# Regrouping the low parts of a Strassen pair's differences, with x's scaling and two weight pieces moved, in a float32 attention and SwiGLU kernel on one NeuronCore

## The chip, the cores and the metric

One core of a Trainium2 chip runs the whole program. The metric is the device time of one execution, in microseconds (us). The kernel before took 1289.45 us, the median of 3 runs (1287.16 to 1290.14).

## What is computed

Two stages follow each other. First, channel attention on q, k and v, each 2 x 6016 x 256 (float32): the columns of q and k are normalised over the 6016 rows, a 256 x 256 score matrix per batch is softmaxed, and v is multiplied by it. Then every one of the 12032 rows of 256 is scaled by its root mean square, multiplied by two 256 x 1536 matrices, gated and projected back:

```
s = kn.T @ qn / tau ; a = softmax(s) ; x = v @ a
xn  = x / rms(x) * rms_g
out = (silu(xn @ w_gate) * (xn @ w_val)) @ w_out
```

Each float32 operand is split into a high part (fp32r) and a low part (the difference to it), and each product is three matmuls: high by high, high by low, low by high.

## The kernel before

**Blocks and steps.** The 12032 rows are worked in 24 blocks (j) of 512 (two are shorter). Blocks 0 and 1 run while scores, norms and weights are still being prepared. A block has 12 steps (f), one per 128 of the 1536 hidden columns; two steps make a pair p = f // 2. From block 2 on, the two matrices into the hidden layer are multiplied by a Winograd scheme of seven products per step, and one step's products are spread over three steps of the program: `emit_step` (from L737) issues for the step two back (`old`) products 7, 2 and 4, for the one before products 3 and 6, and for the new one products 5 and 1. So TensorE's (PE's) order in a step is 7, 2, 3, 6, 5, 1, first half of an output projection, 4, second half. All matmuls of the seven are at L730. A PSUM tile `pu` holds products until VectorE (DVE) and ScalarE (ACT) have read it, and there are three.

**What the other engines do in a step.** ACT copies parts of `pu` into `t` (L766, L771), applies Silu in even steps (L775, L796). DVE adds `pu`, `pq` and `t` into `zg` (even step) or `zv` (odd step) at L759 and L760. In odd steps DVE multiplies gate by value: three quarters at L779, the last quarter, which is product 4, at L788. Then `round_pair` (L653) queues the roundings: ACT makes the high part (L692), GpSimd (POOL) the low part by subtraction (L698). `zg` has two buffers, so a pair's L759 writes over the tile of the pair before the last.

**Turned pairs.** In blocks 4 to 22 the pairs 2, 3 and 4 take the output projection by Strassen's scheme. Their `zg` has four quarters. Three are rounded at once (`gx`); then `run_turned` (L681) makes four differences in place on DVE (L684), in the order quarter 0, 3, 2, 1, after POOL has read the quarters for `gx`. At the start of the next odd step `run_later` (L701) rounds the four differences in two groups, `gy` (quarters 0 and 1) and `gz` (quarters 2 and 3). `G` lists which group's half goes with which weight in the output projection (`emit_out_turned`, L893), which follows about five steps behind. For pair 5, which follows the turned pair 4 and ends in step 1 of the next block, the flag `late` (L777) puts the product of three quarters behind that of the last one, at L790.

**x for the next blocks.** While a block runs, the next block's x is turned by DVE blocks of 32 (L511) and 16 small DMAs on SyncE's (SP's) queue (L520), scaled by `rms_g` on ACT (`scale`, L530), combined on POOL (`parts`, L541 and L546) and rounded in two rounds (`hi` and `rest`, ACT L558 and POOL L560). Tables written by hand (`turn0` to `turn4`, `steady`, with `_mid` and `_pre`) say after which step each is issued: `steady` serves blocks 5 on, `turn2` block 2. `at(j, f, ...)` adds single jobs at the end of a step: softmax pieces of the second batch, and building the Winograd weights (`build_s(p, piece)`: piece 0 and 1 sums and differences on DVE, L578 and L587; 2 rounding on ACT, L590; 3 low parts on DVE, L593). `at_step` holds their steps, counted from block 1's start; those that fall into block 1 are issued inside `emit_hidden`, behind its DVE product at L830.

```
L777  late = old and odd and not strassen(j, f // 2) and strassen(j, f // 2 - 1)
L778  if old and odd and not late:
L779      nc.vector.tensor_tensor(out=zg[:, 1:], in0=zg[:, 1:], in1=z, op=ALU.mult)
L788      nc.vector.tensor_tensor(out=zg[:, 0], in0=u[:, 1], in1=zg[:, 0], op=ALU.mult)
L789      if late:
L790          nc.vector.tensor_tensor(out=zg[:, 1:], in0=zg[:, 1:], in1=z, op=ALU.mult)
```

Of the kernel before, what the change touches and what calls it, by code (L numbers as in the profile page):

```python
# [12 lines left out]
ALU = mybir.AluOpType  # L13
# [6 lines left out]
def kernel(  # L20
# [17 lines left out]
    nc = tc.nc  # L38
# [107 lines left out]
    for b, sizes in enumerate(([2] * 2 + [4] * 9 + [2] * 3 + [1], [CH] * 11 + [3])):  # L146
        t = 0
# [138 lines left out]
    def softmax_exp(b, c):  # L286
        z, mx = sm_t[b]
        nc.scalar.activation(
            out=z[:, c, :], in_=z[:, c, :], func=AF.Exp, scale=-1.0, bias=mx[:, c:c + 1],
            accum_out=mx[:, KC + c:KC + c + 1],  # L290
        )
# [26 lines left out]
    for b in range(B):  # L318
        t = 0
# [6 lines left out]
    B1 = NB // B  # L326
# [316 lines left out]
    rounds, subs, later, turned = [], [], [], []  # L643
# [6 lines left out]
    def by_quarter(t, n, h):  # L650
        return t[:, :n * h].rearrange("p (i n) -> p i n", i=n)

    def round_pair(j, p, zg, h):  # L653

        x, y = new_g("x", 3, j, 2 * p), new_g("y", 2, j, 2 * p + 1)
        engine = nc.vector if (j, p) == (NB - 1, NP - 1) else nc.gpsimd
        w = [[w[:, 2 * p + i, e * P:(e + 1) * P] for w in wo] for i in range(2) for e in range(2)]
        if strassen(j, p):
            z = new_g("z", 2, j, 2 * p + 1)
            a12, a22, a11, s4 = w  # L660
            s1, s2, s3 = ([s[:, PAIRS.index(p), m * P:(m + 1) * P] for s in so_hl] for m in range(3))
            turned.append(zg)
            rounds.append((zg[:, :3], *(by_quarter(t, 3, h) for t in x), engine))
            later.append((zg[:, :2], *(by_quarter(t, 2, h) for t in y), engine))
            later.append((zg[:, 2:], *(by_quarter(t, 2, h) for t in z), engine))
            q = [[t[:, i * h:(i + 1) * h] for t in x] for i in range(3)]
            r = [[t[:, i * h:(i + 1) * h] for t in g] for g in (y, z) for i in range(2)]
            G[j, 2 * p] = [(2, 0, a11, q[0]), (0, 0, a12, q[1]), (0, h, s4, q[2])]
            G[j, 2 * p + 1] = [
                (1, 0, a22, r[1]), (2, h, s2, r[2]), (3, h, s1, r[0]), (3, 0, s3, r[3]),  # L670
            ]
        else:
            rounds.append((zg[:, 1:3], *(by_quarter(t, 2, h) for t in x), engine))
            later.append((zg[:, 0:4:3], *(by_quarter(t, 2, h) for t in y), engine))
            for i, g in enumerate((x, y)):
                if j == NB - 1:
                    G[j, 2 * p + i] = g
                    continue
                G[j, 2 * p + i] = [(e, 0, w[2 * i + e], [t[:, :2 * h] for t in g]) for e in range(2)]
# [7 lines left out]
    def strassen(j, p=PAIRS[0]):  # L687
        return STRA <= j < NB - 1 and p in PAIRS
# [48 lines left out]
    def emit_step(j, f, odd, outs=(), pre=(), mid=()):  # L737
# [5 lines left out]
        now, mid_, old = (flight + [None] * 3)[:3]  # L743
# [3 lines left out]
        if old:  # L747
            j, f, h, product, u, t = old
# [3 lines left out]
            if f % 2 == 0:  # L752
                z = pool["z"].tile([P, 4 * HN], F32, tag="zg", name=f"zg_{j}_{f}")
# [20 lines left out]
        if old and not odd:  # L774
            nc.scalar.activation(out=zg[:, 1:], in_=zg[:, 1:], func=AF.Silu)  # L775
            run_turned()
        late = old and odd and not strassen(j, f // 2) and strassen(j, f // 2 - 1)  # L777
        if old and odd and not late:  # L778
            nc.vector.tensor_tensor(out=zg[:, 1:], in0=zg[:, 1:], in1=z, op=ALU.mult)  # L779
        for go in mid:  # L780
            go()
# [3 lines left out]
        if old:  # L785
            product(4, u[:, 1])
            if odd:
                nc.vector.tensor_tensor(out=zg[:, 0], in0=u[:, 1], in1=zg[:, 0], op=ALU.mult)  # L788
                if late:  # L789
                    nc.vector.tensor_tensor(out=zg[:, 1:], in0=zg[:, 1:], in1=z, op=ALU.mult)  # L790
                round_pair(j, f // 2, zg, h)
                del zs[j, f // 2]
                run_rounds()
                run_subs()
            else:
                nc.scalar.activation(out=zg[:, 0], in_=u[:, 1], func=AF.Silu)  # L796
# [168 lines left out]
    with tc.manual_schedule():  # L965
# [128 lines left out]
        def at(j, f, go):  # L1094
            extra.setdefault((j, f), []).append(go)
# [39 lines left out]
        at(1, 0, lambda: join_squares(1, 1))  # L1135
        at(1, 1, end_scores)
        at_step = [(2 * p + 2, 2 * p + 3, 2 * p + 4, 2 * p + 4) for p in range(NP - 3)]
        at_step += [(8, 9, 10, 12), (13, 14, 15, 16), (16, 18, 19, 20)]
        for i in (2, 3, 0, 1):
            for p in range(NP):  # L1140
                j, f = divmod(NF + at_step[p][i], NF)
# [20 lines left out]
        at(3, 3, lambda: keep_norms(1))  # L1162
        at(5, 2, lambda: softmax_min(1, 0))
        at(6, 2, lambda: softmax_min(1, 1))
        at(7, 2, lambda: (softmax_exp(1, 0), softmax_exp(1, 1)))
        at(B1 - 2, 2, lambda: softmax_div(1, 0))
        at(B1 - 2, 2, lambda: softmax_div(1, 1))

        steps = [(j, f) for j in range(NB) for f in range(NF)]
        owed = []  # L1170
# [21 lines left out]
        def xn(h):  # L1192
            return lambda n: emit_xn(n, h)
# [7 lines left out]
        def of(m, go):  # L1201
# [16 lines left out]
        load = of(3, load_v)  # L1218

        steady = {  # L1220
            1: (s0, scale),
            3: (hi, v1),
            4: (sums_, c0, c1),
            5: (s1,),
# [8 lines left out]
        turn4 = {  # L1233
            **steady,
            1: (v0, s0),
            3: (scale, v1),
            4: (parts, hi, c0, c1),
            5: (rest,),
# [12 lines left out]
            11: (m0, m1),  # L1251
        }
        turn3_mid = {5: (parts,), 7: (x0, q0, r0), 9: (x1, q1), 11: (n1,)}
        turn2_mid = {**turn3_mid, 0: after(1, xn(1))}
        turn2 = {
            **turn3,
            0: after(1, xm(0), xm(1)),
            4: (scale, s0),
            6: (v1,),
            8: (rest,),  # L1260
        }
        turn1 = {
# [96 lines left out]
```

## Time and profile before

| | before |
|---|---|
| median of 3 runs | 1289.45 us (1287.16 to 1290.14) |
| the profiled execution | 1290.91 us, span of its trace 1289.1 us |
| busy: PE, weight loads, DVE, ACT, POOL | 1265.8, 1200.5, 919.2, 853.6, 802.5 us |
| PE's mean granted clock | 0.997 |

The durations below come from the profiled execution. PE's matmuls overlap in the record, so a group of six is shown as one span that is longer than six times the pitch; the end of each is modelled. "Idle" on the weight-load row (PEld) is the time in which the next load waited.

### The profile page before, as it was taken

How to read it: one execution, taken by the hardware profiler on the slowest of the kernel's cores; microseconds unless marked ns; L12 is line 12 of the kernel's file. 1: busy time of each engine (PE TensorE's matmuls, PEld its weight loads, DVE VectorE, ACT ScalarE, POOL GpSimd, SP SyncE). 2: the span in 40 equal slices, each digit the busy share in tenths (PEclk: the TensorE clock that was granted, in tenths of full speed). 3: DMA queues.
4: the chain of work that ended last, by engine and by line, in shares of the span. 5: the costliest groups of instructions: out<-in, count | busy, mean ns of one | idle time of the engine just before them, and what ended most of it. 6: DMA issues, size and time to landing. Idle time of an engine off the chain costs nothing.

```text
span 1289.1 us, 25061 instructions
## 1 busy us (share of the span) xinstructions
PE 1265.8 (98%) x9225; PEld 1200.5 (93%) x9225; DVE 919.2 (71%) x1573; ACT 853.6 (66%) x1771; POOL 802.5 (62%) x639
## 2 busy tenths in 40 slices
PE   8999998999999999999999999999999999999998
PEld 7789987999999999999999999999999999999998
DVE  5789696658667767767777776677677676677664
ACT  5577546666767677666666766766766766766654
POOL 0120254665777777777777766776776776776652
PEclk9999999999999999999999999999999999999999
DMA  8879111120221211211212202202202202101101
GB/s 296 296 233 281 29 34 34 25 40 21 47 33 21 44 27 31 41 26 34 35 22 45 33 18 50 34 17 50 34 18 50 34 18 50 29 18 30 18 1 30
DMA packets 223963, 71.76 MB, mean 56 GB/s; under 512 B 186592, under 2 KB 215392, under 8 KB 223840
## 3 DMA queue, kind: packets, MB, share of 16 engines
q1 hardware_dynamic: 223584, 69.97, 23.5%
q8 instruction: 72, 1.18, 0.4%
q14 instruction: 51, 0.42, 0.1%
q10 hardware_dynamic: 256, 0.20, 0.1%
HBM read 46.40 MB, written 12.32 MB: 46 GB/s over the span
## 4 chain that ended last, share of the span: by engine, by line
PE 62%; DVE 11%; POOL 10%; ACT 5%; DMA 5%; SPq 4%; issue 3%; DVEq 0%; ACTq 0%; POOLq 0%
PE pu L730 27%; PE po L907 16%; POOL gx L698 6%; PE px L435 5%; PE pq L730 4%; PE s L174 4%; SPq L520 4%; DVE zg L684 4%; ACT gx L692 3%; POOL gz L698 3%; DMA raw<-in_k_dram 3%; DMA xnT<-xw 2%; PE po L857 2%; DVE zg L788 1%; DVE zg L779 1%
## 5 line engine op out<-in xcount | busy, mean ns | idle before, releaser
L730 PE MATMUL pu<-xt,w 128*128 128x256 f32 (+1 forms) x2376 | 413.7, 282 | 4.8 <-DVE zg L759 1.4
L730 PE MATMUL pu<-xt,s 128*128 128x256 f32 (+1 forms) x2376 | 367.3, 281 | 4.5 <-ACT t L766 4.5
L730 PEld LDWEIGHTS pu<-xt,w 128*128 128x128 f32 x2376 | 347.4, 189 | 22.9 <-DVE zg L759 8.2
L730 PEld LDWEIGHTS pu<-xt,s 128*128 128x128 f32 x2376 | 327.9, 188 | 18.1 <-ACT t L766 6.0
L698 POOL TENSOR_TENSOR gy<-zg,gy 128x512 fp32r<-128x512 f32 (+1 forms) x131 | 182.3, 1391 | 177.8 <-ACT gy L692 150.6
L698 POOL TENSOR_TENSOR gx<-zg,gx 128x512 fp32r<-128x512 f32 (+2 forms) x131 | 200.5, 1530 | 72.3 <-ACT gx L692 69.9
L771 ACT ACTIVATE t<-pu 128x512 f32<-128x512 f32 (+1 forms) x264 | 156.3, 592 | 86.1 <-PE pu L730 49.6
L907 PE MATMUL po<-gx,w 128*128 128x256 f32 (+1 forms) x927 | 197.1, 331 | 0.0
L779 DVE TENSOR_TENSOR zg<-zg,zv 128x768 f32<-128x768 f32 (+1 forms) x113 | 165.5, 1465 | 12.8 <-ACT gz L692 0.9
L692 ACT ACTIVATE gx<-zg 128x512 fp32r<-128x512 f32 (+2 forms) x132 | 95.1, 720 | 100.6 <-DVE zg L788 53.4
L907 PE MATMUL po<-gy,w 128*128 128x512 f32 (+1 forms) x585 | 157.9, 363 | 0.0
L759 DVE TENSOR_TENSOR zv<-pu,t 128x512 f32<-128x512 f32 (+1 forms) x132 | 89.7, 680 | 81.2 <-ACT zg L796 40.7
L907 PEld LDWEIGHTS po<-gx,w 128*128 128x128 f32 x927 | 136.9, 188 | 5.9 <-ACT os L943 0.2
L766 ACT ACTIVATE t<-pu 128x256 f32<-128x256 f32 (+1 forms) x264 | 99.0, 375 | 64.7 <-PE pu L730 64.4
L684 DVE TENSOR_TENSOR zg<-zg 128x256 f32<-128x256 f32 x228 | 97.0, 425 | 58.6 <-POOL gx L698 52.7
L759 DVE TENSOR_TENSOR zg<-pu,t 128x512 f32<-128x512 f32 (+1 forms) x132 | 90.2, 684 | 66.4 <-POOL gz L698 29.5
L730 PE MATMUL pq<-xt,w 128*128 128x256 f32 (+1 forms) x792 | 136.9, 281 | 0.0
L692 ACT ACTIVATE gy<-zg 128x512 fp32r<-128x512 f32 (+1 forms) x132 | 82.8, 627 | 59.3 <-DVE zg L684 44.4
L788 DVE TENSOR_TENSOR zg<-pu,zg 128x256 f32<-128x256 f32 (+1 forms) x132 | 55.1, 417 | 84.6 <-PE pu L730 73.9
L698 POOL TENSOR_TENSOR gz<-zg,gz 128x512 fp32r<-128x512 f32 x57 | 112.8, 1978 | 0.0
L730 PEld LDWEIGHTS pq<-xt,w 128*128 128x128 f32 x792 | 112.0, 188 | 0.0
L775 ACT ACTIVATE zg<-zg 128x768 f32<-128x768 f32 (+1 forms) x132 | 109.6, 830 | 0.0
(145 smaller groups left out, 2047.4 us busy)
## 6 DMA issues: line engine op xcount, KB each, us to landing
v<-in_v_dram SPq DMA_DIRECT2D x84, 128.0 KB, 3.6
xnT<-xw SPq DMA_DIRECT2D x336, 32.0 KB, 1.9
out_dram<-ob SPq DMA_DIRECT2D x84, 128.0 KB, 3.3
raw<-in_q_dram SPq DMA_DIRECT2D x20, 512.0 KB, 5.9
raw<-in_k_dram SPq DMA_DIRECT2D x20, 512.0 KB, 6.9
wraw<-in_moe_w_gate_dram SPq DMA_DIRECT2D x12, 256.0 KB, 4.4
wraw<-in_moe_w_val_dram SPq DMA_DIRECT2D x12, 256.0 KB, 4.9
wraw<-in_moe_w_out_dram SPq DMA_DIRECT2D x12, 256.0 KB, 5.3
```

The lines of the kernel that those rows point to most:

```text
L435: nc.tensor.matmul(out=px[:, i, :], lhsT=w[:, c, i * P:(i + 1) * P], rhs=x[:, c, :], start=(i == 0 and c == 0 and m == 0), stop=(c == KC - ...
L684: nc.vector.tensor_tensor(out=z[:, o], in0=z[:, i0], in1=z[:, i1], op=ALU.subtract)
L692: nc.scalar.activation(out=gh, in_=hh, func=AF.Copy)
L698: engine.tensor_tensor(out=gl, in0=hh, in1=f32(gh), op=ALU.subtract)
L730: nc.tensor.matmul(out=out, lhsT=wm[wi], rhs=xm[xi], start=(start and q == 0), stop=(q == 2), skip_group_check=True,)
L759: nc.vector.tensor_tensor(out=z[:, 1:], in0=u, in1=t[:, :2], op=ALU.add)
L766: nc.scalar.activation(out=mt[:, 0], in_=mu[:, 1], func=AF.Copy)
L771: nc.scalar.activation(out=nt[:, 1:], in_=nu, func=AF.Copy)
L775: nc.scalar.activation(out=zg[:, 1:], in_=zg[:, 1:], func=AF.Silu)
L779: nc.vector.tensor_tensor(out=zg[:, 1:], in0=zg[:, 1:], in1=z, op=ALU.mult)
L788: nc.vector.tensor_tensor(out=zg[:, 0], in0=u[:, 1], in1=zg[:, 0], op=ALU.mult)
L907: nc.tensor.matmul(out=acc[b][:, o:o + g.shape[-1]], lhsT=w, rhs=g, start=first, stop=True, skip_group_check=True,)
```

## The change

1. The low parts of a turned pair are grouped by the order in which the differences are made: `gy` holds quarters 0 and 3 (made first and second), `gz` quarters 1 and 2. The jobs in `G` are listed anew, with `gy`'s halves first.
2. The flag `late` goes: pair 5 too multiplies its three quarters (L779) ahead of the last.
3. `scale` moves from the end of step 1 to that of step 2 in `steady` (block 4 keeps it at 3). In block 2, `scale` moves from the end of step 4 to step 5, `parts` from the middle of step 5 to the end of step 6, and `hi` from the end of step 5 to that of step 6.
4. Weight pieces: piece 3 of pair 3 (before at block 2, step 0) and piece 0 of pair 4 (before at block 2, step 1) go into block 1's step 11.
5. The second batch's exponentials go from step 2 to step 4 of block 7, and the second half of its softmax division from step 2 to step 3 of block 10.

```
-            later.append((zg[:, :2], *(by_quarter(t, 2, h) for t in y), engine))
-            later.append((zg[:, 2:], *(by_quarter(t, 2, h) for t in z), engine))
+            later.append((zg[:, 0:4:3], *(by_quarter(t, 2, h) for t in y), engine))
+            later.append((zg[:, 1:3], *(by_quarter(t, 2, h) for t in z), engine))
...
-                (1, 0, a22, r[1]), (2, h, s2, r[2]), (3, h, s1, r[0]), (3, 0, s3, r[3]),
+                (3, h, s1, r[0]), (3, 0, s3, r[1]), (1, 0, a22, r[2]), (2, h, s2, r[3]),
...
-        late = old and odd and not strassen(j, f // 2) and strassen(j, f // 2 - 1)
-        if old and odd and not late:
+        elif old:
             nc.vector.tensor_tensor(out=zg[:, 1:], in0=zg[:, 1:], in1=z, op=ALU.mult)
...
-                if late:
-                    nc.vector.tensor_tensor(out=zg[:, 1:], in0=zg[:, 1:], in1=z, op=ALU.mult)
...
-        at_step += [(8, 9, 10, 12), (13, 14, 15, 16), (16, 18, 19, 20)]
+        at_step += [(8, 9, 10, 11), (11, 14, 15, 16), (16, 18, 19, 20)]
...
-        at(7, 2, lambda: (softmax_exp(1, 0), softmax_exp(1, 1)))
+        at(7, 4, lambda: (softmax_exp(1, 0), softmax_exp(1, 1)))
         at(B1 - 2, 2, lambda: softmax_div(1, 0))
-        at(B1 - 2, 2, lambda: softmax_div(1, 1))
+        at(B1 - 2, 3, lambda: softmax_div(1, 1))
...
         steady = {
-            1: (s0, scale),
+            1: (s0,),
+            2: (scale,),
...
         turn4 = {
             **steady,
             1: (v0, s0),
+            2: (),
...
-        turn2_mid = {**turn3_mid, 0: after(1, xn(1))}
+        turn2_mid = {**turn3_mid, 0: after(1, xn(1)), 5: ()}
         turn2 = {
             **turn3,
             0: after(1, xm(0), xm(1)),
-            4: (scale, s0),
-            6: (v1,),
+            4: (s0,),
+            5: (scale,),
+            6: (parts, hi, v1),
             8: (rest,),
```

## Rows read from the trace of the kernel before

**Rows 1.** The page: busy by engine; the chain; L730's loads (busy us, mean ns).

```profile
PE 1265.8 (98%) x9225; PEld 1200.5 (93%) x9225; DVE 919.2 (71%) x1573; ACT 853.6 (66%) x1771; POOL 802.5 (62%) x639
...
PE 62%; DVE 11%; POOL 10%; ACT 5%; DMA 5%; SPq 4%; issue 3%; DVEq 0%; ACTq 0%; POOLq 0%
...
L730 PEld LDWEIGHTS pu<-xt,w 128*128 128x128 f32 x2376 | 347.4, 189 | 22.9 <-DVE zg L759 8.2
```

**Rows 2.** Waits of the weight loads from 358 to 1245 us: total us, times, longest.

```profile
PEld pu L730 <- DVE zg L759: 6.3, 19, 0.4
PEld pu L730 <- ACT t L766: 2.9, 3, 1.0
```

**Rows 3.** Timeline, block 17 step 11, a turned pair: start us, us, engine, what.

```profile
986.64 1.81 DVE L684 TENSOR_TENSOR zg<-zg 128x256 f32<-128x256 f32 x4 [0.41 <-POOL gx L698]
...
987.11 0.52 PE L730 MATMUL pu<-xt,s 128*128 128x256 f32 x3
...
988.49 0.63 ACT L692 ACTIVATE gy<-zg 128x512 fp32r<-128x512 f32 x1 [1.15 <-DVE zg L684]
...
989.25 1.29 POOL L698 TENSOR_TENSOR gy<-zg,gy 128x512 fp32r<-128x512 f32 x1 [2.64 <-ACT gy L692]
...
989.49 1.87 DVE L779 TENSOR_TENSOR zg<-zg,zv 128x768 f32<-128x768 f32 x1
...
990.49 2.02 POOL L698 TENSOR_TENSOR gz<-zg,gz 128x512 fp32r<-128x512 f32 x1
```

**Rows 4.** Timeline, block 18 steps 1 and 2, where pair 5 follows pair 4.

```profile
994.57 0.52 PE L730 MATMUL pu<-xt,s 128*128 128x256 f32 x3
994.62 1.80 DVE L684 TENSOR_TENSOR zg<-zg 128x256 f32<-128x256 f32 x4 [1.05 <-POOL gx L698]
...
997.00 0.61 ACT L692 ACTIVATE gz<-zg 128x512 fp32r<-128x512 f32 x1
...
998.27 1.07 DVE L790 TENSOR_TENSOR zg<-zg,zv 128x768 f32<-128x768 f32 x1
...
998.47 2.03 POOL L698 TENSOR_TENSOR gz<-zg,gz 128x512 fp32r<-128x512 f32 x1
...
999.20 0.87 PE L730 MATMUL pu<-xt,s 128*128 128x256 f32 x6
...
1000.52 0.69 DVE L759 TENSOR_TENSOR zg<-pu,t 128x512 f32<-128x512 f32 x1 [1.19 <-POOL gz L698]
```

**Rows 5.** Timeline, block 9 steps 1 and 2, the same stretch elsewhere.

```profile
554.46 1.30 POOL L698 TENSOR_TENSOR gz<-zg,gz 128x512 fp32r<-128x512 f32 x1
...
554.66 1.91 DVE L790 TENSOR_TENSOR zg<-zg,zv 128x768 f32<-128x768 f32 x1
```

**Rows 6.** Timeline, block 7 steps 2 to 4: the exponentials.

```profile
460.83 1.28 ACT L288 ACT_TABLE_LOAD   x1
...
461.40 0.96 DVE L779 TENSOR_TENSOR zg<-zg,zv 128x768 f32<-128x768 f32 x1
...
464.07 0.50 PE L730 MATMUL pu<-xt,s 128*128 128x256 f32 x2 [0.36 <-ACT t L766]
```

**Rows 7.** Timeline, block 10 steps 2 and 3: the softmax division.

```profile
607.51 0.14 DVE L301 TENSOR_SCALAR mx<-mx 128x1 f32<-128x1 f32 x1
...
611.78 0.68 DVE L759 TENSOR_TENSOR zv<-pu,t 128x512 f32<-128x512 f32 x1
...
612.52 0.63 PE L730 MATMUL pu<-xt,w 128*128 128x256 f32 x3 [1.05 <-DVE zv L759]
```

**Rows 8.** Timeline, block 2 steps 0 to 2: weight pieces on DVE.

```profile
210.00 0.50 PE L730 MATMUL pu<-xt,w 128*128 128x256 f32 x2 [0.92 <-DVE zg L759]
```

**Rows 9.** Timeline, block 2 steps 4 to 6: x's scaling and the wait behind it.

```profile
219.87 1.34 ACT L530 ACTIVATE xnT<-xnT,g_sb 128x512 f32<-128x512 f32 x2 [2.25 <-DMA xnT<-xw]
...
222.57 0.50 PE L730 MATMUL pu<-xt,s 128*128 128x256 f32 x2 [2.04 <-ACT t L766]
```

**Rows 10.** Busy us (instructions) and granted PE clock right behind that wait.

```profile
223.70:227.20 3.50, 3.50 (x16) 3.21 (x15) 2.80 (x6) 2.33 (x5) 3.34 (x4) 0.51 0.01 2
```

## The prediction

> **What bounds it now.** The page comes first: PE is busy 98% of the span, but that counts the time in which a matmul is in flight, and the chain that ended last is PE's own for only 62% [rows 1]. So the gain to be had is PE's waits, and I read them from the weight loads, whose idle time shows a wait that the overlapping matmuls hide. From 358 to 1245 us, the steady blocks, nearly all is two groups [rows 2]: 19 short waits for DVE's L759 on `zg`, 6.3 us in all, and three for ACT's `t`, 2.9 us; a single one for `zv` follows below [rows 7]. In PE's steady stream a matmul of 256 columns has a pitch of 0.118 us (six in 0.87, of which one lasts 0.28 [rows 4]). A load lasts 0.19 us [rows 1] and normally overlaps the one before, so a wait costs its idle time plus 0.07 us: the 19 are worth 6.3 to 7.6 us. I take 7.4.
>
> **Where the 19 come from.** There is one in each of the blocks 5 to 23, in step 2. The reader should follow a turned pair [rows 3]. Offsets are from S, the start of the four differences on DVE. They take 1.81 us together, so two take 0.90. ACT's `gy` starts 0.04 after the fourth (S+1.85), POOL's `gy` 0.76 later (S+2.61), POOL's `gz` 1.24 behind that (S+3.85). DVE's L779 begins at S+2.85 but lasts 1.87, where the same operation lasts 0.96 undisturbed [rows 6]. So it stands for 0.91 us, till S+3.76: 1.15 us into `gy`, before `gz` gets going. `gz` then stands in turn (2.02 against `gy`'s 1.29 [rows 3]). Through the last quarter's product and the rounding this sets the next S: the pairs of rows 3 and 4 are 7.98 us apart, while PE's own two steps take 7.46 (987.11 to 994.57). The chain falls 0.5 us behind with every turned pair, and after pair 4 DVE's L759 of step 2 stands behind POOL's `gz`, whose tile it writes over [rows 4], and PE behind both.
>
> **Parts 1 and 2, grouping and `late`.** No instruction is added. `gy` now needs two differences: ACT at S+0.94, POOL at S+1.70, its port free for DVE at S+2.85, `gz` due at S+2.94. L779 comes at S+2.85 as before, finds the port just free, and ends at S+3.8 instead of S+4.7. That takes 0.9 us from a chain that was 0.5 too long per pair, so PE sets the pace. In step 1 the product of pair 5 goes back to that place: DVE gets L779 about 0.8 us earlier than L790 [rows 4], the last quarter's product stands behind it instead of ahead. With the pair starting some 0.9 us earlier by then, S4 is about 993.7, L779 ends near 997.5 and the quarter is read by 998.3, before PE's product 5 of step 2 wants the bank (second half of the six at 999.20, so 999.55 [rows 4]). `gz` ends near 998.8 instead of 1000.5, and L759 runs on PE's call. The 19 waits go: **-7.4** (0 if something else holds L759 or the bank). The new order of `G` puts `gy`'s matmuls first, in the accumulation five steps behind; both are rounded by then, so nothing.
>
> Who comes first at the port decides this. L790 got it at 998.27 although `gz`'s high part was ready at 997.61 [rows 4]; what counted was who stood there when `gy` let go, and by that row L779 is 0.09 us ahead and the term is -7.4. [...]
>
> **Part 3, `scale`, steady blocks.** Two ACT instructions, 1.3 us [rows 9], move past step 2's copies of `pu` and its Silus. Behind them now stands `gy` of step 3, which finds ACT as late as before, since the copies come 1.3 us earlier. `parts` on POOL still has `gy` ahead of it. In two blocks the 1.3 us were dear: L790 came 0.2 us after `gz` [rows 5] and stood 0.95 for it, so `gx`, `scale` and then `t` came late, about 1.0 us of PE each (two of the three waits for `t` [rows 2]). L790 is gone and `scale` is out of the way: **-2.2** (0 if the median run had none). Blocks 3 and 4 keep their place for `scale`.
>
> **Part 3, block 2.** ACT stood 2.25 us for the DMAs of xnT with `scale` at the end of step 4, and PE 2.0 to 2.3 us for `t` behind it [rows 9]. The 16 DMAs keep their place on SP's queue and land no earlier; at the end of step 5 `scale` meets them without holding step 5's `t`. Its `t` of step 6 comes some 0.9 us before PE wants it, by the same rows: **-2.3**. The clock fell to half right after this wait: 3.50 us at 0.51 [rows 10], with 16 matmuls that count as 19 of 256 columns, 2.2 us at full pitch. Without the wait it should stay up: **-1.3** (0 if the waits at 203 to 210 us suffice to lower it). `parts` (3 POOL) and `hi` (2 ACT, 2 POOL) move past `gx` of step 5; x of block 4 writes the one buffer that `hi` reads, in step 7, so its squares may stand up to 0.6 us on ACT, beside the twelve matmuls of px (1.4 us): nothing on PE.
>
> **Part 4, weight pieces.** In block 2 five DVE instructions delay L759 of step 2, and PE stands 0.9 to 1.1 us [rows 8]. In step 11 of block 1 DVE is idle behind its product, so **-1.1**, but they now run beside POOL's roundings there and the `rr` that x's move waits for. The nearest price of one collision is `gz`'s 0.73 (2.02 less 1.29 [rows 3]); bounds 0 to 1.5, I take **+0.5**.
>
> **Part 5.** The exponentials with their table load (1.28) hold ACT; PE stood 0.36 by its own idle time [rows 6], up to 1.0 by the load's [rows 2]. After step 4 comes the step with px, 1.4 us longer on PE: **-0.6** (0 to -1.0). The division's two halves, 4.27 us of DVE from its first instruction to the late L759, cost PE 1.05 and a little more [rows 7]. Parted, the first fits; the second (2.1) stands before step 4's L759, whose slack no row shows: **-0.6**, the middle between 0 and -1.3.
>
> **The sum.** -7.4 -2.2 -2.3 -1.3 -1.1 +0.5 -0.6 -0.6 = **-15.0**. It is made against the profiled 1290.91 us, 1.46 above the median; the waits are the same in either, so the median goes to 1289.45 - 15.0 = **1274.5 us**. The front of the program, to 200 us, is left as it is and keeps its waits for DMAs.
>
> **Rivals.**
> *`gz` takes the port first (slower).* All of parts 1 and 2 hangs on L779 (S+2.85) coming before `gz` is due (S+2.94): 0.09 us. From that point on the sign turns. If `gz` wins, L779 stands till S+4.09 (`gz` at S+2.94, port free 1.15 later) and ends at S+5.05, later than now (S+4.72). Each pair loses 0.33 more, two of them move S4 to 995.3, and in step 1 the quarter's product would follow L779 at 1000.3 and be done at 1000.7, with product 5 due at 999.55. PE loses some 1.2 us per block instead of 0.39: 19 x 0.8 = +15, less the other parts' 7.6: **1297**. For it: rows 5, where POOL's `gz` was 0.2 earlier and DVE stood 0.95. Against it: in rows 3 and 4 DVE stood or came there 0.2 to 1.0 us before `gz` started and got the port both times, in rows 4 with `gz` ready first. [...] Chance 0.10.
> *The stall only changes its name.* L779 ahead of the quarter delays the release of the bank, or L759 finds another reader, and the 19 waits stay at their size. The rest gives 7.6: **1282**. For it: the quarter's product loses its lead. Chance 0.15.
> *Block 2's wait moves, not goes.* xnT's DMAs, set off later by the collision, land so late that step 6 or 7 stands instead, and the clock falls all the same: 3.6 less, **1278**. Chance 0.12.
> *The change does nothing measurable,* within 0.2% (2.6 us, about what a measurement of this kernel can tell): every wait is replaced. Chance 0.03.
>
> **Numbers.** The forecast has 0.60, at 1274.5. Its own range by the bounds above is 1272 to 1279. The range for 8 in 10 takes in the third rival and most of the second: **1271 to 1282**. Faster: 0.60 + 0.15 + 0.12 = 0.87; same 0.03; slower 0.10.
>
> **What would show it.** Right: in turned pairs ACT's `gy` starts about 0.95 us after S instead of 1.85, L779 lasts about 1.0; the weight loads' waits for L759 of `zg` fall from 19 to nearly none; the granted clock near 224 us does not fall; PE's period per block falls by about 0.4 us. Wrong: L779 at 2.2 us, or waits of `pu` for L788 in step 2; ACT idle for xnT in step 5 with PE standing behind it; a new wait at step 4 of block 10.

## The result, and the profile after

| | before | after |
|---|---|---|
| median (range), 6 runs each, same chip | 1288.84 us (1287.09 to 1290.14) | 1274.57 us (1273.29 to 1278.96) |
| ratio after / before, 95% interval | | 0.9896 [0.9879, 0.9914] |
| profiled execution, span of its trace | 1290.91, 1289.1 us | 1273.29, 1271.5 us |

The changed kernel is faster by 14.3 us between the medians; the interval of the ratio makes that 11 to 16 us. The two profiled executions differ by 17.6 us. Of these, 1.4 lie in the front, where the change does nothing but for the weight pieces at its end: PE's granted clock fell to 0.51 to 0.64 from 56 to 60 us in the profile of before, and stayed at 1.00 there in that of after. From the last output projection of block 1, where PE waits for POOL's `gz` (203.34 us before, 201.93 after), to the end the two differ by 16.2 us, against 15.0 in the prediction's sum.

Both traces hold 9225 matmuls in the same order, but for `G`'s jobs, so the start of the n-th in one can be set against the n-th in the other. By this count 5.0 of the 16.2 us arise in block 2, none in blocks 3 and 4, and 11.2 behind them. "Matmul by matmul" below means this comparison of two traces.

The page of the changed kernel, busy time by engine and the chain that ended last:

```profile
PE 1256.1 (99%) x9225; PEld 1197.0 (94%) x9225; DVE 884.6 (70%) x1573; ACT 869.9 (68%) x1771; POOL 802.4 (63%) x639
...
PE 95%; DMA 2%; DVE 1%; ACT 1%; issue 0%; POOL 0%; SPq 0%; POOLq 0%; DVEq 0%; ACTq 0%
```

The busy shares have hardly moved [rows 1]. The chain has: PE's own share goes from 62% to 95%, and DVE, POOL and ACT have all but left it. DVE is busy 35 us less with the same 1573 instructions: the product of three quarters (L779 and L790 before, L778 after) takes 148.8 us in its 132 instructions where it took 187.4, since it stands less beside POOL. What the prediction calls the port is read from such times, and means no more than they show of this product and POOL's L698: L779, started beside `gy`, lasted 1.87 us instead of 0.96, and `gz`, started beside L779, lasted 2.02 instead of 1.29 [rows 3, 6].

The waits of the weight loads from 345 to 1245 us, changed kernel (us in all, times, longest), answer to [rows 2]. The list leaves out idle times that are shorter than those it shows:

```profile
PEld pu L730 <- ACT zg L793: 0.5, 1, 0.5
PEld pu L730 <- DVE zg L759: 0.4, 1, 0.4
```

The 19 waits for L759 and the two long waits for `t` are gone. What stays is one wait behind the exponentials and one at the softmax division (both below). Lines behind the old L777 are one to three lower after the change: L779 is now L778, L788 is L787, L796 is L793.

A turned pair of the changed kernel in the timeline (block 17, step 11), which answers to [rows 3]:

```profile
971.29 1.81 DVE L684 TENSOR_TENSOR zg<-zg 128x256 f32<-128x256 f32 x4 [0.66 <-POOL gx L698]
...
972.08 0.51 PE L730 MATMUL pu<-xt,s 128*128 128x256 f32 x3
972.21 0.63 ACT L692 ACTIVATE gy<-zg 128x512 fp32r<-128x512 f32 x1
...
972.98 1.29 POOL L698 TENSOR_TENSOR gy<-zg,gy 128x512 fp32r<-128x512 f32 x1 [1.72 <-PE pq L730]
...
974.13 0.96 DVE L778 TENSOR_TENSOR zg<-zg,zv 128x768 f32<-128x768 f32 x1
...
974.22 2.03 POOL L698 TENSOR_TENSOR gz<-zg,gz 128x512 fp32r<-128x512 f32 x1
...
979.54 0.51 PE L730 MATMUL pu<-xt,s 128*128 128x256 f32 x3
```

Read each start against S = 971.29. ACT's `gy` begins at S+0.92 (before S+1.85), POOL's `gy` at S+1.69 (S+2.61), L778 at S+2.84 as before, but it takes 0.96 us instead of 1.87, and `gz` starts 0.09 us behind it and stands in its turn (2.03 us). PE's two steps take 7.46 us (972.08 to 979.54), DVE's next differences after 7.48 (the next ones start at 978.77), where they were 7.98 apart before. The chain no longer falls behind PE.

Block 2, behind x's scaling, timeline and a window of the changed kernel (us, then busy us and instructions of PE, PEld, DVE, ACT and POOL, the granted clock, DMA share, GB/s), which answer to [rows 9, 10]:

```profile
218.61 1.34 ACT L530 ACTIVATE xnT<-xnT,g_sb 128x512 f32<-128x512 f32 x2
...
221.59 0.51 PE L730 MATMUL pu<-xt,s 128*128 128x256 f32 x3
```

```profile
222.00:226.00 4.00, 4.00 (x33) 3.87 (x33) 3.83 (x6) 2.01 (x5) 3.92 (x5) 1.00 0.84 130
```

`scale` finds its data and does not stand (2.25 us before), PE's step 6 starts without a wait (2.04 before), and the clock stays at 1.00 (0.51 before).

Earlier in block 2, around the moved weight pieces, changed kernel, which answers to [rows 8]:

```profile
202.32 1.14 POOL L464 TENSOR_TENSOR rr<-ss,mhalf 128x2 f32<-128x2 f32 x1
...
203.49 0.84 ACT L476 ACTIVATE xn<-px,rr 128x256 f32<-128x256 f32 x2 [1.08 <-POOL rr L464]
...
205.63 0.62 PE L730 MATMUL pu<-xt,s 128*128 128x256 f32 x3 [0.84 <-ACT t L766]
```

The wait for L759 (0.92 by PE's idle time, 1.13 by the load's) is gone. In exchange POOL's `rr` takes 1.14 us, where it took 0.72 in the trace of before, beside the weight piece that now runs on DVE; ACT's `xn` and then `t` come later, and PE's wait for `t` in step 2 grows from 0.47 to 0.84 us. A second wait for L759, two steps on, is gone as well; the rows did not have it. In the trace of before:

```profile
215.62 0.41 PEld L730 LDWEIGHTS pu<-xt,w 128*128 128x128 f32 x3 [0.29 <-DVE zg L759]
```

Matmul by matmul the two waits are worth 1.6 us and the collision costs 0.4.

### The profile page after: what moved, and what is told of

Same layout as the page of the kernel before. It is cut to its first block, busy times and chain, and to the rows that moved or that the text cites. A ratio compares the mean times of both kernels' runs of the same rounds, so it can differ in the third digit from the quotient of the medians.

```text
span 1271.5 us, 25137 instructions
## 1 busy us (share of the span) xinstructions
PE 1256.1 (99%) x9225; PEld 1197.0 (94%) x9225; DVE 884.6 (70%) x1573; ACT 869.9 (68%) x1771; POOL 802.4 (63%) x639
## 4 chain that ended last, share of the span: by engine, by line
PE 95%; DMA 2%; DVE 1%; ACT 1%; issue 0%; POOL 0%; SPq 0%; POOLq 0%; DVEq 0%; ACTq 0%
PE pu L730 44%; PE po L904 26%; PE pq L730 7%; PE px L435 5%; PE s L174 5%; PE po L854 3%; DMA raw<-in_k_dram 2%; PE pg L813 2%; PE pv L813 2%; PE warm L987 0%; POOL rr L464 0%; DVE wx L122 0%; ACT xn L476 0%; PE pxt L498 0%; SPq L160 0%
## 5 line engine op out<-in xcount | busy, mean ns | idle before, releaser
L730 PE MATMUL pu<-xt,w 128*128 128x256 f32 (+1 forms) x2376 | 410.7, 281 | 0.4 <-DVE zv L759 0.3
L730 PE MATMUL pu<-xt,s 128*128 128x256 f32 (+1 forms) x2376 | 366.0, 280 | 1.1 <-ACT t L766 0.8
L730 PEld LDWEIGHTS pu<-xt,w 128*128 128x128 f32 x2376 | 347.2, 189 | 13.9 <-DVE zv L759 1.0
L730 PEld LDWEIGHTS pu<-xt,s 128*128 128x128 f32 x2376 | 326.9, 188 | 13.5 <-ACT t L766 1.0
L698 POOL TENSOR_TENSOR gy<-zg,gy 128x512 fp32r<-128x512 f32 (+1 forms) x131 | 182.0, 1389 | 149.7 <-ACT gy L692 83.2
L698 POOL TENSOR_TENSOR gx<-zg,gx 128x512 fp32r<-128x512 f32 (+2 forms) x131 | 200.7, 1532 | 87.6 <-ACT gx L692 85.5
L759 DVE TENSOR_TENSOR zv<-pu,t 128x512 f32<-128x512 f32 (+1 forms) x132 | 89.7, 680 | 103.0 <-ACT zg L793 76.7
L778 DVE TENSOR_TENSOR zg<-zg,zv 128x768 f32<-128x768 f32 (+1 forms) x132 | 148.8, 1127 | 14.4 <-DVE zv L760 0.5
L730 PE MATMUL pq<-xt,w 128*128 128x256 f32 (+1 forms) x792 | 137.3, 281 | 0.0
L787 DVE TENSOR_TENSOR zg<-pu,zg 128x256 f32<-128x256 f32 (+1 forms) x132 | 55.6, 421 | 95.6 <-PE pu L730 94.8
L759 DVE TENSOR_TENSOR zg<-pu,t 128x512 f32<-128x512 f32 (+1 forms) x132 | 89.0, 674 | 43.9 <-PE pu L730 29.3
L904 PE MATMUL po<-gy,w 128*128 128x512 f32 x414 | 118.4, 394 | 0.0
L698 POOL TENSOR_TENSOR gz<-zg,gz 128x512 fp32r<-128x512 f32 x57 | 112.8, 1980 | 0.0
L730 PEld LDWEIGHTS pq<-xt,w 128*128 128x128 f32 x792 | 112.2, 188 | 0.0
L174 PE MATMUL s<-raw 128*128 128x256 f32 x376 | 86.5, 383 | 7.0 <-DMA raw<-in_k_dram 7.0
```

Source lines behind the costliest of these rows:

```text
L174: nc.tensor.matmul(out=s_ps[b][:, c, :], lhsT=r[:, 1, t, c * P:(c + 1) * P], rhs=r[:, 0, t, :], start=(t0 + t == 0 and c == 0), stop=(t0 + ...
L698: engine.tensor_tensor(out=gl, in0=hh, in1=f32(gh), op=ALU.subtract)
L730: nc.tensor.matmul(out=out, lhsT=wm[wi], rhs=xm[xi], start=(start and q == 0), stop=(q == 2), skip_group_check=True,)
L759: nc.vector.tensor_tensor(out=z[:, 1:], in0=u, in1=t[:, :2], op=ALU.add)
L904: nc.tensor.matmul(out=acc[b][:, o:o + g.shape[-1]], lhsT=w, rhs=g, start=first, stop=True, skip_group_check=True,)
```

## The experiments

Eleven kernels ran. Five are the kernel before with one part of the change, one is the changed kernel with one part undone, and five put small operations on DVE into the changed kernel, to bring about or to price what the slower rival said. Ratios are to the kernel before on the same chip in the same set of runs, with the 95% interval.

| run | what it is | median us | ratio to before |
|---|---|---|---|
| e1_group | before + grouping | 1281.79 | 0.9940 [0.9921, 0.9959] |
| e2_late | before + `late` removed | 1287.28 | 0.9978 [0.9969, 0.9988] |
| e5_turn2 | before + block 2's tables | 1287.29 | 0.9974 [0.9964, 0.9984] |
| e6_weights | before + weight pieces | 1290.76 | 1.0007 [0.9990, 1.0025] |
| e8_soft | before + part 5 | 1288.92 | 0.9991 [0.9979, 1.0003] |
| e7_scaleback | after, steady `scale` back in step 1 | 1275.40 | 0.9883 [0.9861, 0.9904] |
| e3_gzfirst | after, 2 small operations ahead of L778's product | 1275.01 | 0.9885 [0.9868, 0.9902] |
| e4_behind | after, 2 behind it | 1276.05 | 0.9889 [0.9872, 0.9905] |
| e9_four | after, 4 ahead of it | 1297.46 | 1.0056 [1.0036, 1.0076] |
| e10_fourbehind | after, 4 behind it | 1275.19 | 0.9885 [0.9860, 0.9910] |
| e11_once | after, 4 ahead, once a block | 1275.93 | 0.9890 [0.9869, 0.9912] |

### Grouping alone

```
-            later.append((zg[:, :2], *(by_quarter(t, 2, h) for t in y), engine))
-            later.append((zg[:, 2:], *(by_quarter(t, 2, h) for t in z), engine))
+            later.append((zg[:, 0:4:3], *(by_quarter(t, 2, h) for t in y), engine))
+            later.append((zg[:, 1:3], *(by_quarter(t, 2, h) for t in z), engine))
```

(and `G`'s jobs listed anew; `late` stays).

> The kernel before with part 1 alone (low parts grouped by order of making; the flag late stays). My theory: the order at the shared port between gy and gz lengthens the chain of turned pairs, and the grouping alone cures it. ACT's gy at S+0.94, L779 about 1.0 us in pairs 3 and 4; L790 comes when gy has long let go. The 19 waits for L759 of zg go (6.3 us of idle loads to under 1), and with them the blocks in which L790 met gz: 7 to 10 us less than before, 1279 to 1282. Rival (the flag late carries the gain): the 19 waits stay, 0 to 2 us less, 1287 to 1289.

The gain is 0.60% of the time, 7.7 us (5.3 to 10.2), and the 19 waits leave the list. Waits of the weight loads from 350 to 1260 us:

```profile
PEld pu L730 <- ACT t L766: 2.1, 4, 0.9
PEld pu L730 <- DVE zg L759: 0.3, 1, 0.3
```

In step 1 of the next block L790, still behind the last quarter, runs undisturbed, since `gz` has come and gone by then:

```profile
988.37 1.29 POOL L698 TENSOR_TENSOR gz<-zg,gz 128x512 fp32r<-128x512 f32 x1
...
989.91 0.95 DVE L790 TENSOR_TENSOR zg<-zg,zv 128x768 f32<-128x768 f32 x1
```

The two long waits for `t`, about 1.0 us each before, have not gone: they are 0.39 us each, in the same two blocks, and one of 0.47 at 1091.57 us is new.

The 7.7 us are not the 19 waits alone, though. Matmul by matmul this trace is 9.4 us shorter than that of before from block 2 on. Of these, 2.2 lie in block 2, which this edit does not touch. In most of the 19 blocks the lead grows by 0.20 us, where the changed kernel gains 0.35, so the 19 are worth about 4.7 us here. The two long waits give 1.5. And 1.3 come from the softmax division: its wait, in the list of before from 358 to 1245 us

```profile
PEld pu L730 <- DVE zv L759: 1.5, 1, 1.5
```

is not in the list of this run, though both halves still stand in step 2. L759 of that step is no longer late, so the division starts in time (e1_group):

```profile
600.56 0.68 DVE L759 TENSOR_TENSOR zg<-pu,t 128x512 f32<-128x512 f32 x1
...
601.49 0.14 DVE L301 TENSOR_SCALAR mx<-mx 128x1 f32<-128x1 f32 x1
```

Before, L759 stood 1.19 us for `gz` there, as in [rows 4], and the division behind it.

### `late` removed alone

```
-        late = old and odd and not strassen(j, f // 2) and strassen(j, f // 2 - 1)
-        if old and odd and not late:
+        elif old:
...
-                if late:
-                    nc.vector.tensor_tensor(out=zg[:, 1:], in0=zg[:, 1:], in1=z, op=ALU.mult)
```

> The kernel before with part 2 alone (late removed, grouping as before). My theory: L779 of pair 5 now stands behind gy like those of pairs 3 and 4 (1.9 us), the quarter's product comes later, gz ends when it did, so the 19 waits stay at 0.3 to 0.5 us each; at most the two long waits for t go: 2 us less to 3 us more than before, 1287 to 1292. Rival (the flag late carries the gain): the 19 waits go, 7 us less, 1282.

It gains 0.22% (2.8 us, 1.5 to 4.0). The waits of the weight loads from 350 to 1260 us show that the 19 do not go, they change their name:

```profile
PEld pu L730 <- DVE zg L787: 4.0, 19, 0.4
PEld pu L730 <- DVE zv L759: 1.6, 2, 1.5
PEld pu L730 <- ACT t L766: 0.8, 1, 0.8
```

The timeline of one of the 19:

```profile
994.38 1.87 DVE L778 TENSOR_TENSOR zg<-zg,zv 128x768 f32<-128x768 f32 x1
...
995.40 2.01 POOL L698 TENSOR_TENSOR gz<-zg,gz 128x512 fp32r<-128x512 f32 x1
...
996.14 1.12 PE L730 MATMUL pu<-xt,s 128*128 128x256 f32 x6
996.18 0.41 DVE L787 TENSOR_TENSOR zg<-pu,zg 128x256 f32<-128x256 f32 x1
```

With the old grouping L778 still stands for 0.91 us, and the last quarter's product (L787), which reads PE's `pu`, now stands behind it. PE's six matmuls, for which it needs that tile back, take 1.12 us instead of 0.87. This is the second rival (the stall only changes its name), and it is what `late` does by itself; only with the grouping is L778 short enough. The 4.0 us of idle loads are less than the 6.3 of before, but matmul by matmul the 19 cost the same under either name, to 0.03 us in nearly every block. The two long waits for `t` are gone here, however: 1.1 us each.

### `scale` back in step 1 of the steady blocks

```
         steady = {
-            1: (s0,),
-            2: (scale,),
+            1: (s0, scale),
```

(with it the empty entry for step 2 that block 4's table needed; block 2's own tables as in the changed kernel).

> The changed kernel with scale put back to step 1 in blocks 5 on. My theory: the two long waits for t came from L790 behind gz, which is gone, so scale's move is worth nothing beside parts 1 and 2: within 1 us of the changed kernel, no wait of PE for t in step 3, 1273.5 to 1276. Rival (the move of scale carries its own 2.2 us or more): 1276.5 or above, with waits for t in steps 2 or 3.

1275.40 us is the changed kernel's time again, and its weight loads show the same two small waits as the changed kernel's, none for `t`. Matmul by matmul it is 0.2 us shorter than the changed kernel from block 2 on. The steady blocks' move of `scale` is worth nothing that these runs can see, once the two other parts are in. The move alone on the kernel before was not tried.

### Block 2's tables alone, and the weight pieces alone

Block 2's tables alone (`scale` from step 4 to 5, `parts` and `hi` to step 6):

```
-        turn2_mid = {**turn3_mid, 0: after(1, xn(1))}
+        turn2_mid = {**turn3_mid, 0: after(1, xn(1)), 5: ()}
...
-            4: (scale, s0),
-            6: (v1,),
+            4: (s0,),
+            5: (scale,),
+            6: (parts, hi, v1),
```

> The kernel before with block 2's tables alone (scale at the end of step 5, parts and hi at the end of step 6). My theory: PE's wait for t before step 6 (2.0 to 2.5 us) goes and the clock does not fall: 3 to 4 us less than before, 1285 to 1286. Rival (the wait only moves): a wait of like size for t in step 7 or for xnT, clock low for 3.4 us as before: 0 to 1 us less, 1288 to 1289.

It gains 0.26%: 3.35 us (2.1 to 4.6), where the prediction had 2.3 + 1.3 = 3.6. The wait ahead of step 6 is gone, and the clock stays up through the stretch:

```profile
218.00:226.00 8.00, 8.00 (x59) 7.51 (x59) 6.94 (x13) 6.14 (x12) 7.84 (x8) 1.00 0.46 106
```

The weight pieces alone:

```
-        at_step += [(8, 9, 10, 12), (13, 14, 15, 16), (16, 18, 19, 20)]
+        at_step += [(8, 9, 10, 11), (11, 14, 15, 16), (16, 18, 19, 20)]
```

> The kernel before with part 4 alone (two weight pieces in block 1's step 11). My theory: the wait for L759 in block 2's step 2 (1.1 us) goes, but POOL's rounding and rr stand for the pieces, x's DMAs start about 0.5 us later, and without the new tables PE waits for xnT before step 6 all the longer, which takes the gain back: 0 to 0.7 us more than before, 1288.8 to 1289.5. Rival (the terms add): 0.6 to 1.1 us less, 1287.7 to 1288.2.

1.0007 [0.9990, 1.0025]: no gain. The profiled execution took 1297.99 us against a median of 1290.76, and most of what it takes more than that of before lies in the front: the last output projection of block 1 waits for `gz` at 209.25 us, where before it was 203.34. What is read here is block 2 alone. The wait for L759 in step 2 goes here too, but ACT's wait for x's DMAs, with PE's wait for `t` behind it, grows from 2.25 and 2.04 us to:

```profile
226.14 1.33 ACT L530 ACTIVATE xnT<-xnT,g_sb 128x512 f32<-128x512 f32 x2 [3.85 <-DMA xnT<-xw]
...
228.84 1.01 PE L730 MATMUL pu<-xt,s 128*128 128x256 f32 x3 [3.63 <-ACT t L766]
```

Counted from that projection, `scale` gets its data 0.4 us later than before (16.9 us against 16.5), and PE arrives at step 6 1.2 us earlier (16.0 against 17.2): what PE saves in step 2 it waits for the DMAs. The granted clock is 0.50 to 0.53 from 228 to 234 us. Matmul by matmul block 2 is 1.1 us longer than before. So the two edits are not additive: the weight pieces pay only where block 2's tables have given `scale` room. Part 4's term of the prediction (-1.1 +0.5) is there beside the rest of the change, not by itself.

### Part 5 alone

```
-        at(7, 2, lambda: (softmax_exp(1, 0), softmax_exp(1, 1)))
+        at(7, 4, lambda: (softmax_exp(1, 0), softmax_exp(1, 1)))
...
-        at(B1 - 2, 2, lambda: softmax_div(1, 1))
+        at(B1 - 2, 3, lambda: softmax_div(1, 1))
```

> The kernel before with part 5 alone (exponentials at step 4, the division's second half a step on). From the traces of the two kernels: the exponentials' waits fall from 0.9 to 0.5 us, the division's from 1.3 to about 0.3: 1.2 to 1.5 us less than before, 1287.3 to 1287.6. Rival (the second half of the division costs at step 4 what it saved): 0.4 us less or nothing.

0.9991 [0.9979, 1.0003]: the expected gain of about 1 us fits, and so does none. The trace of this run says more. Matmul by matmul it gains 0.8 us behind block 2, 0.6 at the exponentials and 0.3 at the division, not the 1.2 to 1.5 expected. The division's wait has moved: the second half now stands before step 4's L759, and PE waits there (e8_soft; it was 1.05 us in step 3 [rows 7]):

```profile
611.04 0.10 DVE L301 TENSOR_SCALAR mx<-mx 128x1 f32<-128x1 f32 x1
...
613.82 0.63 PE L730 MATMUL pu<-xt,w 128*128 128x256 f32 x3 [0.76 <-DVE zg L759]
```

So the rival, that the second half costs at step 4 what it saved, came true in the main.

In the changed kernel both stretches look like this. The exponentials bring two table loads on ACT, one ahead of them and one that takes ACT back to Silu two steps later:

```profile
459.67 1.28 ACT L288 ACT_TABLE_LOAD   x1
...
468.14 1.28 ACT L775 ACT_TABLE_LOAD   x1
...
470.60 0.62 PE L730 MATMUL pu<-xt,s 128*128 128x256 f32 x3 [0.27 <-ACT zg L793]
```

By the weight loads' idle time PE waited 0.80 us behind the first load and 0.19 behind the second in the trace of before; now it is nothing and 0.47. The division's first half starts at 595.75 and meets no wait. Its second half:

```profile
602.55 0.11 DVE L301 TENSOR_SCALAR mx<-mx 128x1 f32<-128x1 f32 x1
...
604.21 0.68 DVE L759 TENSOR_TENSOR zg<-pu,t 128x512 f32<-128x512 f32 x1
```

L759 of `zg` comes 1.7 us behind the first instruction of this half, where the two halves together took 4.27 up to theirs. PE's wait there is 0.4 us of the weight loads (the one in the list above), 0.25 matmul by matmul.

### The slower rival, forced

The forecast hung on 0.09 us: L778's product arrives at S+2.85, and POOL's `gz` is due at S+2.94. To make `gz` come first, small operations on a tile of their own (128x1) were put on DVE ahead of the product in the odd steps behind turned pairs, three places a block:

```
+            if strassen(j, f // 2 - 1):
+                for _ in range(2):
+                    nc.vector.tensor_scalar(
+                        out=ticks[0], in0=ticks[0], scalar1=1.0, scalar2=None, op0=ALU.mult
+                    )
             nc.vector.tensor_tensor(out=zg[:, 1:], in0=zg[:, 1:], in1=z, op=ALU.mult)
```

(the tile is made and set to 1 once, at the start).

> The changed kernel with two tiny DVE operations (128 x 1) ahead of L779 in the steps that follow a turned pair, so that L779 comes after gz has been due (S+2.94). My theory (order at the port decides): L779 lasts about 1.9 us and ends at S+5.05, pairs are 8.28 us apart instead of about 7.5, PE waits 0.8 to 1.2 us in each of 19 blocks: 15 to 22 us more than the changed kernel, 1290 to 1297. Rival (0.4 us of DVE's time costs nothing, DVE is off the path now): within 2 us of the changed kernel, 1273 to 1277.

It missed its aim. In the timeline (S = 971.94) the two mostly fill the time between L761 (the old L760), which makes the product's input, and the product:

```profile
974.26 0.41 DVE L761 TENSOR_TENSOR zv<-pq,t 128x256 f32<-128x256 f32 x1
...
974.59 0.33 DVE L781 TENSOR_SCALAR tick<-tick 128x1 f32<-128x1 f32 x2
...
974.84 0.95 DVE L784 TENSOR_TENSOR zg<-zg,zv 128x768 f32<-128x768 f32 x1
974.87 2.06 POOL L698 TENSOR_TENSOR gz<-zg,gz 128x512 fp32r<-128x512 f32 x1
```

The product (now L784) starts at S+2.90, 0.05 us later than without them, and still 0.03 ahead of `gz`. It got the port and ran in 0.95 us. The run says nothing on the rival's price, but it narrows the point from which it decides. Its control, the two behind the product, costs nothing either and so tells nothing:

> The changed kernel with the same two tiny DVE operations behind L779 instead of ahead of it, ahead of the last quarter's product. My theory: L779 still comes at S+2.85 and gets the port; the quarter's product waits for PE's product 4 anyway; within 1 us of the changed kernel, 1273.5 to 1276. Rival (what costs in the run with them ahead is the added DVE work, not the port): as that run, 15 us or more above the changed kernel.

With four of them (`range(4)`) at the same place:

> As the run with two tiny operations ahead of L779, but four: with two, L779 began at S+2.90 and still got the port 0.03 us ahead of gz, so that run did not test the loss. Four put it at S+3.2 or later, behind gz (S+2.94). My theory (a lost port three times per block): L779 lasts some 1.7 us, ends at S+5.05, turned pairs are 8.3 us apart where PE needs 7.5, PE waits 0.8 to 1.1 us per block: 15 to 21 us above the changed kernel, 1290 to 1296. Rival (the chain has slack by now, as at 672 us in the changed kernel, where L779 lost once and no wait of PE followed): less than 3 us above, 1275 to 1278.

1297.46 us (1294.37 to 1298.80), slower than before, ratio 1.0056 [1.0036, 1.0076], and 22.3 us over its control below. The timeline of a turned pair (S = 993.80):

```profile
993.80 1.80 DVE L684 TENSOR_TENSOR zg<-zg 128x256 f32<-128x256 f32 x4 [1.34 <-POOL gx L698]
...
995.49 1.30 POOL L698 TENSOR_TENSOR gy<-zg,gy 128x512 fp32r<-128x512 f32 x1 [1.72 <-ACT gy L692]
...
996.46 0.71 DVE L781 TENSOR_SCALAR tick<-tick 128x1 f32<-128x1 f32 x4
...
996.74 1.29 POOL L698 TENSOR_TENSOR gz<-zg,gz 128x512 fp32r<-128x512 f32 x1
...
997.08 1.76 DVE L784 TENSOR_TENSOR zg<-zg,zv 128x768 f32<-128x768 f32 x1
...
998.77 0.41 DVE L793 TENSOR_TENSOR zg<-pu,zg 128x256 f32<-128x256 f32 x1
...
999.23 0.63 PE L731 MATMUL pu<-xt,s 128*128 128x256 f32 x3 [0.45 <-DVE zg L793]
```

Now `gz` starts at S+2.94 and runs undisturbed (1.29), L784 stands and ends at S+5.04. The rival said S+2.94 and S+5.05. Two such pairs follow each other at 8.30 us (the pair before starts its differences at 985.50), where the rival had 7.98 + 0.33. The weight loads of this run from 350 to 1260 us, two waits in nearly each block:

```profile
PEld pu L731 <- DVE zg L793: 18.5, 37, 0.7
```

With 0.07 us on top of each, as in the prediction, this is 21 us, 1.1 for each of 19 blocks; the rival had 1.2. Matmul by matmul e9 falls 22.0 us behind its control. The second wait of a block is the one at 999.23 above, behind the third lost port. The first is behind the second lost port, one pair earlier than the rival had it:

```profile
990.93 0.41 PEld L731 LDWEIGHTS pu<-xt,s 128*128 128x128 f32 x3 [0.33 <-DVE zg L793]
```

The control, four behind the product:

> The same four tiny operations behind L779, ahead of the last quarter's product: the same DVE work, no lost port. My theory: the quarter's product comes 0.1 to 0.4 us later, which the slack of the chain takes: within 2 us of the changed kernel, 1274 to 1277. Rival (the added DVE work counts, wherever it stands): as the run with four ahead.

1275.19 us, as without any. So the 0.71 us of four operations on DVE cost under 1 us (0.9 matmul by matmul against the changed kernel). In e9 the four also delay the product by 0.43 us, which no run has without the lost port. Without the 0.81 us for which it stood the product would end at S+4.23. Before, it ended at S+4.72 with pairs 7.98 us apart, so this makes about 7.5 per pair, PE's own pace: an estimate from these rows, by which the lost port is what turned the delay into 22 us.

Four ahead of the product, but only behind the first turned pair of a block (`and f // 2 == PAIRS[0] + 1`), so one lost port a block:

> Four tiny operations ahead of L779 only in the step behind pair 2, so that the port is lost once per block instead of three times. My theory (losses add up from pair to pair against a slack of some 0.4 to 0.8 us): one loss puts the next pair 8.3 us behind the last and the following ones catch up; no wait of PE, within 2 us of the changed kernel, 1274 to 1277. Rival (every loss costs alike): a third of what the run with four in all three steps costs.

1275.93 us: nothing that shows. The chain makes up for one lost port before PE needs it; in e9 PE waits from the second in a row on. From block 5 on the changed kernel loses the port twice by itself behind a turned pair, at 675 and 1128 us, where L778 comes 0.2 and 0.4 us late. The first of them, where it was an L759 that ran late:

```profile
672.12 1.80 DVE L684 TENSOR_TENSOR zg<-zg 128x256 f32<-128x256 f32 x4 [1.25 <-POOL gx L698]
...
675.05 1.29 POOL L698 TENSOR_TENSOR gz<-zg,gz 128x512 fp32r<-128x512 f32 x1
...
675.18 1.98 DVE L778 TENSOR_TENSOR zg<-zg,zv 128x768 f32<-128x768 f32 x1
...
680.40 0.89 DVE L684 TENSOR_TENSOR zg<-zg 128x256 f32<-128x256 f32 x2 [0.77 <-POOL gx L698]
```

L778 came 0.13 us behind `gz` and stood for 1.0 us; the next differences follow after 8.28 us, and no PE wait comes of it.

## Why the prediction came out right, and where it did not

**Parts 1 and 2, -7.4: right, mechanism and size.** In the turned pair every offset is within 0.03 us of the one forecast: ACT's `gy` S+0.92 (0.94 forecast), POOL's `gy` S+1.69 (1.70), L778 S+2.84 (2.85) for 0.96 us, `gz` S+2.93 (2.94). From block 5 on all turned pairs but two keep to these offsets within 0.06 us. All 19 waits are gone, and matmul by matmul they are worth 7.3 us. That the grouping by itself gives 7.7 (5.3 to 10.2) is no second proof of the 7.4: in e1's trace 4.7 of it are the 19, and the rest are other waits. The 0.15 us a block that it leaves go when `late` goes too. That the product would find the port free since it stands there first was read from [rows 4]; e3 and e9 show it on both sides: 0.03 us ahead of `gz` the product ran in 0.95 us, and 0.34 us behind it (996.74 to 997.08) it took 1.76. In both the one that started first ran at its undisturbed length. To be ready first did not count: in e3 `gz`'s high part was there at 974.46 (973.83 + 0.63), 0.38 us ahead of the product's start, and the product got the port.

**Part 3 in the steady blocks, -2.2: the size right, the step wrong.** The two long waits for `t` are gone, but not since "`scale` is out of the way": with `scale` back in step 1 (e7) they stay away. What takes them out is L778 ahead of the last quarter (e2, with neither the grouping nor the move: 1.1 us each); the grouping alone leaves 0.39 us of each (e1), since L790 then comes when `gz` has gone. The other half of that sentence, "L790 is gone", was the cause. So this term belongs to parts 1 and 2.

**What `late` does was seen only with its partner.** The prediction put the bank's release down as safe, and as a rival if it was not. e2 shows that rival coming true without the grouping: 19 waits, for L787 instead of L759. In the changed kernel it doesn't come, because the product ahead is 0.9 us shorter. The argument for it (L778's end near 997.5, the quarter read in time) was therefore right, but it rested on part 1.

**Part 3 in block 2, -2.3 -1.3: right.** Step 6's wait is gone, the clock doesn't fall, and e5 measures 3.35 us (2.1 to 4.6) for the 3.6. Matmul by matmul the wait is worth 2.3 us and the clock 1.5. Both depend on the execution: in e1 and e8, which have the same program up to there, this wait was 1.41 and 1.10 us instead of 2.04, the clock did not fall behind it (1.00 in both), and block 2 was 2.2 and 2.5 us shorter than in the profile of before. So part of the 3.6 is there in some executions with the old tables and not in others.

**Part 4, -1.1 +0.5: right in kind, half the size, and not alone.** The wait of 0.92 to 1.13 us is gone, and with it the second one, of 0.29 by the loads, that the prediction did not count: 1.6 us matmul by matmul. The collision costs 0.37 (the wait for `t`) and 0.05 (the wait for `gz` before it): +0.42. The price of the collision was taken from another one of its kind and lay 0.08 too high. So the part is worth 1.2 us instead of 0.6. That the edit needs block 2's tables (e6) was not in the prediction: without them PE only comes earlier to the same DMAs.

**Part 5, -0.6 -0.6: the sum nearly right, the division's share not part 5's.** The exponentials gave about 0.35. The step with px does cover their own table load, as forecast; what stays is the load that takes ACT back to Silu, behind which PE's wait grows from 0.19 to 0.47 us. In e8, with the old grouping, they gave the 0.6. The division's stretch is 1.05 us shorter, but it is the grouping that shortens it: e1, with both halves in step 2, has it 1.3 us shorter, and e8, with the halves parted but the old grouping, 0.3. What made the division dear in [rows 7] was the late L759 ahead of it, one of the 19. The first half fits, as forecast; step 4's L759, whose slack no row showed, has too little for the second (PE stands 0.76 us there in e8, and 0.25 matmul by matmul in the changed kernel). Beside the grouping, parting the halves rather costs 0.25 us.

**The sum.** Matmul by matmul the 16.2 us are: the 19 waits 7.3, the two long waits 2.2, block 2's wait 2.3, the clock there 1.5, part 4 1.2, the exponentials 0.35, the division 1.05, and 0.3 at the very end of the program, which no term has. So the prediction's sum was 1.2 too small for the execution that it was made from, part 4, the division and the end being most of that. Its step to the median took the waits to be the same in either, which block 2 of e1 and e8 does not bear out, and the medians differ by 14.3 (11 to 16). That 1274.5 meets the measured 1274.57 is in part luck.

**The slower rival** had its price right: 1297 was worked out, and e9, which brings its condition about, took 1297.46 (1294.37 to 1298.80). Its decision point was right to 0.1 us: won at S+2.90 (e3), lost at S+3.06 (672.12 to 675.18). It had one wait per block, behind the third lost port; e9 has two, the first behind the second. What it did not say is that a single lost port is not paid for at all (e11).

**Left open.** In the kernel before, blocks 9 and 13 had the long waits for `t`, and in the changed kernel two pairs, at 672 and 1125 us, had L778 0.2 and 0.4 us late. What makes DVE late at just these places was not found.

## What to carry to other kernels

Where two engines take turns at one resource within a chain, ask who stands there when it comes free, with starts counted from the head of the chain: here 0.09 us lay between the forecast and a loss that, forced in three pairs a block, cost 22 us, and no busy share showed it. Group results in the order in which they are made, so that the engine behind can begin on the first group. When a rival hangs on such a margin, push it over on purpose and look in the trace whether it really fell; a run whose push was too small says nothing of the price. And ask of every term which other part of the change it needs: run alone, part 2 kept its 19 waits, part 4 gained nothing, and the division's gain came without the edit that was meant for it.

## What the runs showed of the hardware that was not expected

- Two 128x1 operations on DVE that the product does not depend on, 0.33 us as recorded, put ahead of it moved it by 0.05 us; four, 0.71 us as recorded, moved it to S+3.28, by 0.43 (e3, e9). The product otherwise starts 0.51 us behind the start of the operation that makes its input (973.62 to 974.13 in the changed kernel), and the first two fit into that time.
- In e9 the product got going ahead of `gz`'s recorded end, by an estimate from its times: L784 ends at 998.84; less its undisturbed 0.95 it got going at 997.89, which is 1.15 us behind the start of a `gz` whose record lasts 1.29. The prediction had the same 1.15 from [rows 3].
- At the same place of block 2 the granted clock of PE was 0.52 behind a wait of 1.83 us (e2, 224 to 226 us), 0.50 behind one of 2.04 us (before, 224 to 226 us) and 0.50 at the end of one of 3.63 us (e6, 228 to 230 us; 0.76 from 226 to 228, within the wait). It was 1.00 behind waits of 1.41 us (e1, 222 to 226 us) and 1.10 us (e8, 222 to 226 us). These five waits are all that the runs show of it there.
